# Gated mix of two attentions: the first 512 positions in halves of three tiles, other first loads, and rows whose three parts lie side by side

## The chip, the cores and the metric

The kernel runs on one core of a Trainium2 chip. The metric is the device time of one execution in microseconds (us), as the median of several runs. Engines are named as the profile names them: PE (TensorE, matrix products), PEld (its weight loads), DVE (VectorE), ACT (ScalarE), POOL (GpSimd) and SP (SyncE, which here only issues transfers). A `q` behind an engine's name is its instruction queue. DMA transfers move data between the chip's main memory (DRAM) and the on-chip memory, in which a tile has 128 partitions.

## The reference, cut to what matters

```
x: [2048, 576]; H = 32 heads of Dh = 18
g = sigmoid((x * gate_w).sum(-1))
A: q, k, v = split(x @ wqkv)              # every head has its own q, k, v
   a = concat_heads(softmax(q k^T / sqrt(18)) v) @ wo
B: q = x @ wq;  k = x @ wk;  v = x @ wv   # one k and one v for all 32 heads
   b = concat_heads(softmax(q k^T / sqrt(18)) v) @ wo
out = g * a + (1 - g) * b
```

All of it is in 32-bit floats, with 2048 positions. The two attentions make 64 heads; heads 0 to 31 (B) share one key, heads 32 to 63 (A) have their own.

## The kernel before, in words

**Precision.** A 32-bit value is cut into a high and a low part, each of a format (fp32r) that PE multiplies in one pass. A product of two values is made of three products of parts: high by high, low by high and high by low. For the scores, the parts stand as rows of one matmul: a query's 18 rows three times (high, high, low) and a key's (high, low, high), which gives 54 rows; two further rows carry the row maximum and ones. Each such block is kept twice in a tile, at partitions 0 (`SB`, used for the scores) and 64 (`MB`, used for the search for the maximum), so that PE can work with both halves at once. `load_rows` (line 89) brings these blocks from the DRAM tensor `qk_d`, in six transfers of 18 rows: three parts, twice.

**First phase, the projections.** `wall` holds all weights for keys, gate, shared values and queries as 14 tiles of 128 columns (`MT`); `xT` is x transposed. x and each weight tile have 576 rows; they lie as 5 k-tiles, of which the first four are full and the fifth has 64 rows, held twice (high in the upper half of the partitions, low in the lower). `PROJ` lists the 14 products for one output tile: 4 high by high, 4 low by high, 4 high by low, and 2 on the fifth k-tile. `project(mt, c, w)` makes the tile `mt` for the 512 positions of chunk `c`: 14 matmuls into a PSUM bank (`ps_s`, three banks), then ACT copies the high part, DVE subtracts for the low part, and POOL issues the transfer to `qk_d`. Tile 0 (shared key, gate, shared values) also keeps a plain copy `pst`. For tiles with keys, chunk 1 also gives the difference of keys of chunk 1 and chunk 0 (`pdhl`), written to `kd_d`; in the search for the maximum ACT takes the positive part of what it gives, and DVE adds that to the scores of chunk 0, so that one pass of DVE gives the maximum over both chunks.

**Start.** `load5` loads a block of five k-tiles in three transfers: the first four k-tiles, then the fifth twice, into the two halves. The first weight tile and the first 256 positions of x go out on SP, with their small transfers on ACT (`rest`); then the second 256 positions, weight tiles 1 and 2, and the rest of x in pieces of 512, all on SP. Two pieces of 512 fit at a time; the third waits for the first to be split. PE multiplies dummy data six times meanwhile (line 246). `first_x` (line 215) splits the first weights and the first 256 positions, `split_x` (line 227) any later 256: ACT copies all five k-tiles for the high part, DVE subtracts four for the low part (`low_x`, line 236) and the lower half of the fifth (line 237). Then chunk 0 is made: tile 0 in two halves of 256 positions, tile 1, tile 2; and the same for chunks 1 to 3, each with the splitting of the next 512 positions behind tile 1 and with `shared_v` (four transposes on PE, a copy on DVE) before tile 2. `project_rest` (line 283) makes tiles 3 to 13 and issues, one per call of `project`, the list `rows_back` of first key and query loads.

**Second phase.** For 64 heads and 16 blocks of 128 keys: `step_max` searches the maximum 22 steps ahead, `step_scores` makes the scores and ACT their exponentials, `step_pv` multiplies with the values. The order of all instructions is written out by hand (`manual_schedule`, the strings `PLAIN`, `SPARSE`, `DENSE`, `ALONE`); each engine and each queue works through its own in that order. `load_q`, `load_k` and `next_kd` (`load_kd`, line 97: three transfers of 18 rows) are put on SP at steps given by `when`.

Of the kernel before, what the change touches and what calls it, by code (L numbers as in the profile page):

```python
# [8 lines left out]
F32 = mybir.dt.float32  # L9
# [15 lines left out]
MT = 14  # L25
# [17 lines left out]
def gated_mix_kernel(ctx: ExitStack, tc: tile.TileContext, xT, wall, wv, wo, out):  # L43
# [3 lines left out]
    def dma(o, i, eng=None):  # L47
        o, i = (x.bitcast(F32) if x.dtype == F32R else x for x in (o, i))
        return (eng or nc.sync).dma_start(o, i)
# [91 lines left out]
    def project(mt, c, w, parts=1):  # L141


        fp = ps_s.tile([P, 512], F32, name="ps")
        cs = slice(c * 512, (c + 1) * 512)
        g = 512 // parts
        for i in range(parts):
            for n, (a, b, k, kr) in enumerate(PROJ):
                nc.tensor.matmul(fp[:, g * i:g * i + g], w[a][:kr, k, :],  # L149
                                 X[b][:kr, k, c * 512 + g * i:c * 512 + g * i + g],  # L150
                                 start=(n == 0), stop=(n == len(PROJ) - 1))
        hl = stp.tile([P, 2, 512], F32R, name="phl", bufs=4)
        nc.scalar.activation(hl[:, 0, :], fp, AF.Copy)  # L153
# [5 lines left out]
        nc.vector.tensor_tensor(hl[:, 1, :], fp, hl[:, 0, :].bitcast(F32), op=OP.subtract)  # L159
        dma(qk_d[:, mt * P:(mt + 1) * P, cs].rearrange("a p f -> p a f"), hl, nc.gpsimd)  # L160
        if c == 1 and mt in HAS_K:
            d = stp.tile([P, 512], F32, name="pd", bufs=1)
            nc.vector.tensor_tensor(d, fp, KD.pop(mt), op=OP.subtract)
            dhl = stp.tile([P, 2, 512], F32R, name="pdhl", bufs=1)
            split(d, dhl[:, 0, :], dhl[:, 1, :], nc.scalar, nc.vector)
            dma(kd_d[:, mt * P:(mt + 1) * P, :].rearrange("a p f -> p a f"), dhl, nc.gpsimd)
        if mt == 0:
            dma(z_d[cs], st[ROW_G:ROW_G + 1, :])
            return c, st

    def shared_v(c, st):
        pv = ps_m.tile([P, 512], F32, name="pm")
        for j in range(4):
            nc.tensor.transpose(pv[:, 18 * j:18 * j + 18],  # L174
                                st[ROW_VB:ROW_VB + 18, j * P:(j + 1) * P],
                                ident[ROW_VB:ROW_VB + 18, ROW_VB:ROW_VB + 18])
        nc.vector.tensor_copy(vb[:, 4 * c:4 * c + 4, 0:18],
                              pv[:, 0:72].rearrange("p (j d) -> p j d", d=18))
# [28 lines left out]
    with tc.tile_pool(name="xs", bufs=1, side="right") as xsp:  # L207
        XS = []

        def load_x(c, rest=None):  # L210
            half = c < 2
            XS.append(xsp.tile([P, NKT, 256 if half else 512], F32, name="xsh" if half else "xs", bufs=2))
            load5(XS[c], xT[:, 256 * c:256 * c + 256] if half else xT[:, 512 * (c - 1):512 * c], rest)

        def first_x():

            xs, xh = XS[0], X["h"][:, :, 0:256]
            w = {y: wpool.tile([P, NKT, P], F32R, name=f"w{y}", bufs=3) for y in "hl"}
            st = W.pop(0)
            nc.scalar.activation(w["h"], st, AF.Copy)  # L220
            nc.vector.tensor_copy(xh[:, 0:3], xs[:, 0:3])
            nc.scalar.activation(xh[:, 3:5], xs[:, 3:5], AF.Copy)  # L222
            nc.vector.tensor_tensor(w["l"], st, w["h"].bitcast(F32), op=OP.subtract)
            low_x(0, xs)
            return w

        def split_x(c):
            xs = XS[c // 2 + 1][:, :, 256 * (c % 2):256 * (c % 2) + 256] if c > 1 else XS[c]
            cs = slice(c * 256, (c + 1) * 256)
            nc.scalar.activation(X["h"][:, :, cs], xs, AF.Copy)  # L230
            low_x(c, xs)

        def low_x(c, xs):
            cs = slice(c * 256, (c + 1) * 256)
            xh = X["h"][:, :, cs]
            nc.vector.tensor_tensor(X["l"][:, :, cs], xs[:, 0:4], xh[:, 0:4].bitcast(F32), op=OP.subtract)
            nc.vector.tensor_tensor(xh[64:128, 4], xs[64:128, 4], xh[64:128, 4].bitcast(F32), op=OP.subtract)

        W = [load_w(0, nc.scalar)]
        load_x(0, nc.scalar)  # L240
        nc.scalar.activation(ones, ones, AF.Copy)
        load_x(1)

        warm = ps_m.tile([P, 512], F32, name="pm")
        for i in range(6):
            nc.tensor.matmul(warm[:, 0:304], ident, vb.rearrange("p k d -> p (k d)"), start=True, stop=True)
        W.append(load_w(1))
        W.append(load_w(2))
        for c in range(2, 5):
            load_x(c)  # L250
        dma(ones_r.rearrange("a (b c) -> (a b) c", c=32), ones)
        for mt in range(3, 6):
            W.append(load_w(mt))
        for t in vst:
            nc.gpsimd.memset(t, 1.0)
        WP = [first_x()]
        split_x(1)
        WP.append(prep_w(W.pop(0)))
        WP.append(prep_w(W.pop(0)))
        for c in range(4):  # L260
            keep = project(0, c, WP[0], 2 if c == 0 else 1)
            if c == 3:
                WN = prep_w(W.pop(0))
            project(1, c, WP[1])
            if c < 3:
                split_x(2 * c + 2)
                split_x(2 * c + 3)
            shared_v(*keep)
            project(2, c, WP[2])
    vwp = ph1.enter_context(tc.tile_pool(name="vwp", bufs=1, side="right"))  # L270

    def load_wv(hf):
# [540 lines left out]
```

## Time and profile before

| | before |
|---|---|
| median of 3 runs | 2756.39 us (2756.0 to 2756.66) |
| the profiled execution | 2756.49 us, span 2754.5 us |
| granted TensorE clock, mean | 0.999 |
| HBM read, written | 137.23 MB, 64.77 MB |
| packets on SP's and ACT's transfers, on POOL's | 108880 and 4928, 9504 |

A row of the table of stretches gives a stretch's bounds and length, then for each engine its busy time in it and the number of its instructions, then the granted clock, the mean busy share of the DMA engines and what they moved in GB/s. A row of the timeline gives the start, the duration, the engine with the line of the kernel, the operation, the tile written and the tiles read, and in brackets how long the engine had been idle and what released it. A row of the chain of waits gives start, duration and what held the end back at that time. A matmul's end is modelled, so starts of successive groups are the better measure of its pace.

### The profile page before, as it was taken

What the parts mean: (1) busy time and instruction counts of PE and PEld (TensorE: products, weight loads), DVE (VectorE), ACT (ScalarE), POOL (GpSimd) and SP (SyncE); (2) the same over time, 40 slices, a digit from 0 to 9 for tenths busy, and PEclk for the clock granted to TensorE, in tenths of its full rate; (3) what the DMA queues carried; (4) which work ended last, traced back from release to release, by engine and by line L of the source; (5) the groups of instructions that cost most, each with busy time, mean ns of one, the idle gap of its engine ahead of it and who ended that gap; (6) DMA issues with size and microseconds to landing.
All of it is one profiled execution on the core that took longest, in us unless ns stands there. A gap on an engine that the chain in (4) does not pass through costs nothing.

```text
span 2754.5 us, 59149 instructions
## 1 busy us (share of the span) xinstructions
PE 2744.5 (100%) x22926; PEld 1264.5 (46%) x22926; DVE 2414.4 (88%) x4518; ACT 2432.4 (88%) x4777; POOL 209.3 (8%) x339
## 2 busy tenths in 40 slices
PE   9999999999999999999999999999999999999999
PEld 7888333333333333333334444444444333334554
DVE  4347999999999999999999898888989999998873
ACT  3332999999999999999999999999999999998776
POOL 2220000001000100100110001000100011011000
PEclk9999999999999999999999999999999999999999
DMA  8652011112112111211133323322331233234312
GB/s 265 251 218 72 24 33 27 32 43 66 37 27 57 51 33 35 62 48 28 52 94 107 83 58 96 93 67 77 100 87 47 66 86 97 67 75 123 110 36 88
DMA packets 123592, 214.61 MB, mean 78 GB/s; under 512 B 53516, under 2 KB 81628, under 8 KB 111626
## 3 DMA queue, kind: packets, MB, share of 16 engines
q1 hardware_dynamic: 108880, 171.05, 22.9%
q0 software_dynamic: 9504, 34.61, 3.3%
q10 hardware_dynamic: 4928, 5.18, 0.5%
q8 instruction: 180, 2.95, 0.5%
q14 instruction: 100, 0.82, 0.1%
HBM read 137.23 MB, written 64.77 MB: 73 GB/s over the span
## 4 chain that ended last, share of the span: by engine, by line
PE 99%; DMA 0%; DVE 0%; ACT 0%; issue 0%; SPq 0%
PE acc L430 39%; PE ps L417 37%; PE pm L382 9%; PE ps L149 7%; PE pm L565 4%; PE ps L185 2%; PE pm L417 0%; PE ps L382 0%; DMA xsh<-xT 0%; DVE oacc L574 0%; DMA wst<-wall 0%; DVE mx L391 0%; ACT pt L424 0%; PE ps L619 0%; PE pm L174 0%
## 5 line engine op out<-in xcount | busy, mean ns | idle before, releaser
L424 ACT ACTIVATE pt<-ps 128x512 f32<-128x512 f32 x4052 | 2131.5, 613 | 106.5 <-PE pm L382 45.0
L391 DVE TENSOR_REDUCE mx<-pm 128x1 f32<-128x512 f32 x3064 | 1946.9, 684 | 141.1 <-PE pm L382 100.5
L417 PE MATMUL ps<-qs,ksb 56*128 56x512 f32 x2688 | 905.8, 437 | 0.3
L382 PE MATMUL pm<-ksb,qs 54*128 54x512 f32 x2332 | 806.7, 441 | 0.0
L417 PEld LDWEIGHTS ps<-qs,ksb 56*128 56x128 f32 x2688 | 436.8, 184 | 643.7 <-ACT pt L424 622.8
L430 PE MATMUL acc<-pt,vb 128*19 128x256 f32 (+1 forms) x6144 | 592.4, 457 | 0.0
L430 PE MATMUL acc<-pt,vg 128*19 128x256 f32 (+3 forms) x6432 | 573.9, 443 | 0.5 <-DVE oe L442 0.4
L417 PE MATMUL ps<-qs,ksa 56*128 56x512 f32 x1364 | 453.5, 437 | 0.1
L382 PE MATMUL pm<-ksa,qs 54*128 54x512 f32 x1232 | 425.5, 438 | 0.0
L382 PEld LDWEIGHTS pm<-ksb,qs 54*128 54x128 f32 x2332 | 373.7, 184 | 34.8 <-DVE mx L391 15.2
L388 DVE CUSTOM_DVE_ANT_0 junk<-pm,xb 128x512 bf16<-128x512 f32 x500 | 340.3, 681 | 1.3 <-ACT xb L385 1.2
L417 PEld LDWEIGHTS ps<-qs,ksa 56*128 56x128 f32 x1364 | 218.3, 184 | 245.9 <-ACT pt L424 216.4
L385 ACT ACTIVATE xb<-pm 128x512 f32<-128x512 f32 x500 | 306.2, 612 | 0.0
L382 PEld LDWEIGHTS pm<-ksa,qs 54*128 54x128 f32 x1232 | 197.9, 184 | 56.3 <-DVE mx L391 25.9
L430 PEld LDWEIGHTS acc<-pt,vg 128*19 128x19 f32 x6432 | 122.3, 97 | 216.1 <-issue 190.4
L430 PEld LDWEIGHTS acc<-pt,vb 128*19 128x19 f32 x6144 | 104.3, 97 | 209.5 <-issue 199.0
L382 PE MATMUL pm<-kdb,qs 54*128 54x512 f32 x372 | 150.6, 405 | 0.0
L115 POOL CAST mh<-mt 128x32 fp32r<-128x32 f32 x64 | 13.4, 210 | 1729.1 <-DVE mt L399 1729.0
L153 ACT ACTIVATE phl<-ps 128x512 fp32r<-128x512 f32 x56 | 33.5, 598 | 102.9 <-PE ps L149 74.0
L159 DVE TENSOR_TENSOR phl<-ps,phl 128x512 fp32r<-128x512 f32 x56 | 38.7, 692 | 93.7 <-ACT phl L153 70.9
L149 PE MATMUL ps<-xh,wh 128*128 128x512 f32 (+1 forms) x285 | 83.5, 390 | 2.5 <-ACT xh L222 1.8
L149 PE MATMUL ps<-xh,wl 128*128 128x512 f32 (+1 forms) x285 | 82.7, 388 | 0.0
(118 smaller groups left out, 1370.7 us busy)
## 6 DMA issues: line engine op xcount, KB each, us to landing
qs<-qk SPq DMA_DIRECT2D x384, 144.0 KB
qk<-phl POOLq DMA_DIRECT2D x56, 512.0 KB, 4.3
ksa<-qk SPq DMA_DIRECT2D x132, 144.0 KB
ksb<-qk SPq DMA_DIRECT2D x66, 144.0 KB
onh<-oh SPq DMA_DIRECT2D x32, 256.0 KB
onl<-ol SPq DMA_DIRECT2D x32, 256.0 KB
oih<-onh SPq DMA_DIRECT2D x16, 512.0 KB
oil<-onl SPq DMA_DIRECT2D x16, 512.0 KB
```

The source lines that it names most:

```text
L149: nc.tensor.matmul(fp[:, g * i:g * i + g], w[a][:kr, k, :], X[b][:kr, k, c * 512 + g * i:c * 512 + g * i + g], start=(n == 0), stop=(n == ...
L153: nc.scalar.activation(hl[:, 0, :], fp, AF.Copy)
L159: nc.vector.tensor_tensor(hl[:, 1, :], fp, hl[:, 0, :].bitcast(F32), op=OP.subtract)
L185: nc.tensor.matmul(fp[:, 0:288], X[b][:kr, k, st_ * P:(st_ + 1) * P], w[a][:kr, k, :], start=(n == 0), stop=(n == len(PROJ) - 1))
L382: nc.tensor.matmul(pm, qs[u % 3][b:b + 54, i * P:(i + 1) * P], k, start=True, stop=True)
L385: nc.scalar.activation(MX["x", u, i], pm, AF.Relu)
L388: nc.vector.tensor_tensor_reduce(junk, pm, MX.pop(("x", u, i)), 1.0, -3e38, op0=OP.add, op1=OP.max, accum_out=MX[u][:, i, c:c + 1])
L391: nc.vector.tensor_reduce(MX[u][:, i, c:c + 1], pm, axis=AX.X, op=OP.max)
L417: nc.tensor.matmul(ps, kst(u)[b:b + 56, i * P:(i + 1) * P], qs[u % 3][b:b + 56, c * 512:(c + 1) * 512], start=True, stop=True)
L424: nc.scalar.activation(pt, ps, AF.Exp, scale=SCALE)
L430: nc.tensor.matmul(acc[32 * j:32 * j + 19, a:b], v_of(u, i), PT[u, i, j][:, a:b], start=(i == 0), stop=(i == 15), skip_group_check=True)
L565: nc.tensor.matmul(fp[:, 0:288], x, y, start=(n == 0 and not joins), stop=(n == len(ops) - 1))
```

## The change

There are three edits.

1. **First loads.** Weight tiles 1 and 2 now come ahead of the second 256 positions of x, and the two small transfers of the fifth k-tile of each of these three (`rest`) are issued by POOL instead of SP. The large transfers stay on SP.
2. **First 512 positions.** The splitting of the first three weight tiles and of the first 256 positions is cut into "the first four k-tiles" (`main_w`, first half of the x split, `low_x`) and "the fifth" (`last_w`, `last_x`), and ordered so that the former of all three tiles come first. `project` is cut into `products` (matmuls n0 to n1 of the list) and `leave` (the rest). Chunk 0 is then made with three banks at once: products 0 to 11 for the first 256 positions of tiles 0, 1, 2, then products 12 and 13 of these, then the second 256 positions tile by tile. Tile 0 of chunk 1, instead of chunk 0, is made in two halves.
3. **Rows.** In a block of 54 rows the three parts of a row now lie side by side (row 3d + part instead of 18 part + d): `load_rows` still issues six transfers of 18 rows, each to every third partition. `kd_d` holds the three parts of a row next to each other, so `load_kd` is one transfer of 54 rows; it is written with two transfers (two parts, then the first again) in place of one.

```diff
-    kd_d = dram.tile([2, MT * P, 512], F32, name="kd")
+    kd_d = dram.tile([MT * P, 3, 512], F32, name="kd")
...
-                put(t[b + 18 * i:b + 18 * i + 18, :], qk_d[y, r:r + 18, :])
+                put(t[b + i:b + 54:3, :], qk_d[y, r:r + 18, :])
...
     def load_kd(t, r, put=dma):
-        for i, y in enumerate((0, 1, 0)):
-            put(t[MB + 18 * i:MB + 18 * i + 18, :], kd_d[y, r:r + 18, :])
+        put(t[MB:MB + 54, :], kd_d[r:r + 18, :, :].rearrange("p a f -> (p a) f"))
...
+    def products(fp, w, x0, p0, g, n0=0, n1=len(PROJ)):
+        for n, (a, b, k, kr) in list(enumerate(PROJ))[n0:n1]:
+            nc.tensor.matmul(fp[:, p0:p0 + g], w[a][:kr, k, :], X[b][:kr, k, x0 + p0:x0 + p0 + g],
+                             start=(n == 0), stop=(n == len(PROJ) - 1))
...
-            dma(kd_d[:, mt * P:(mt + 1) * P, :].rearrange("a p f -> p a f"), dhl, nc.gpsimd)
+            dma(kd_d[mt * P:(mt + 1) * P, 0:2, :], dhl, nc.gpsimd)
+            dma(kd_d[mt * P:(mt + 1) * P, 2, :], dhl[:, 0, :], nc.gpsimd)
...
-        def first_x():
...
+        def main_w(st):
+            w = {y: wpool.tile([P, NKT, P], F32R, name=f"w{y}", bufs=3) for y in "hl"}
+            nc.scalar.activation(w["h"][:, 0:4], st[:, 0:4], AF.Copy)
+            nc.vector.tensor_tensor(w["l"][:, 0:4], st[:, 0:4], w["h"][:, 0:4].bitcast(F32), op=OP.subtract)
             return w
+        def last_w(st, w):
+            nc.scalar.activation(w["h"][:, 4], st[:, 4], AF.Copy)
+            nc.vector.tensor_tensor(w["l"][:, 4], st[:, 4], w["h"][:, 4].bitcast(F32), op=OP.subtract)
...
         W = [load_w(0, nc.scalar)]
         load_x(0, nc.scalar)
         nc.scalar.activation(ones, ones, AF.Copy)
-        load_x(1)
+        W.append(load_w(1, nc.gpsimd))
+        W.append(load_w(2, nc.gpsimd))
+        load_x(1, nc.gpsimd)
...
-        W.append(load_w(1))
-        W.append(load_w(2))
         for c in range(2, 5):
             load_x(c)
...
-        WP = [first_x()]
+        x0, xh = XS[0], X["h"][:, :, 0:256]
+        ST = [W.pop(0) for _ in range(3)]
+        WP = [main_w(ST[0])]
+        nc.scalar.activation(xh[:, 0:2], x0[:, 0:2], AF.Copy)
+        nc.vector.tensor_copy(xh[:, 2:4], x0[:, 2:4])
+        low_x(0, x0)
+        WP.append(main_w(ST[1]))
+        WP.append(main_w(ST[2]))
+        last_w(ST[0], WP[0])
+        nc.scalar.activation(xh[:, 4], x0[:, 4], AF.Copy)
+        last_x(0, x0)
+        last_w(ST[1], WP[1])
+        last_w(ST[2], WP[2])
         split_x(1)
-        WP.append(prep_w(W.pop(0)))
-        WP.append(prep_w(W.pop(0)))
+        FP = [ps_s.tile([P, 512], F32, name="ps") for _ in range(3)]
+        for n in ((0, 12), (12, 14)):
+            for mt in range(3):
+                products(FP[mt], WP[mt], 0, 0, 256, *n)
         for c in range(4):
-            keep = project(0, c, WP[0], 2 if c == 0 else 1)
...
+            for mt in range(3):
...
+                if c == 0:
+                    products(FP[mt], WP[mt], 0, 256, 256)
+                    done = leave(mt, c, FP[mt])
+                else:
+                    done = project(mt, c, WP[mt], 2 if c == 1 and mt == 0 else 1)
```

More of the change, by code (lines that the diff above doesn't have):

```diff
@@ L144, in project, with leave @@
         fp = ps_s.tile([P, 512], F32, name="ps")
-        cs = slice(c * 512, (c + 1) * 512)
         g = 512 // parts
         for i in range(parts):
[L148 to L151, printed above, removed]
+            products(fp, w, c * 512, g * i, g)
+        return leave(mt, c, fp)
+    def products(fp, w, x0, p0, g, n0=0, n1=len(PROJ)):
+        for n, (a, b, k, kr) in list(enumerate(PROJ))[n0:n1]:
+            nc.tensor.matmul(fp[:, p0:p0 + g], w[a][:kr, k, :], X[b][:kr, k, x0 + p0:x0 + p0 + g],
+                             start=(n == 0), stop=(n == len(PROJ) - 1))
+    def leave(mt, c, fp):
+        cs = slice(c * 512, (c + 1) * 512)
         hl = stp.tile([P, 2, 512], F32R, name="phl", bufs=4)
@@ L231, in split_x, with last_x @@
             low_x(c, xs)
+            last_x(c, xs)
         def low_x(c, xs):
             cs = slice(c * 256, (c + 1) * 256)
[L235 to L237 removed]
+            nc.vector.tensor_tensor(X["l"][:, :, cs], xs[:, 0:4], X["h"][:, 0:4, cs].bitcast(F32), op=OP.subtract)
+        def last_x(c, xs):
+            xh = X["h"][64:128, 4, c * 256:(c + 1) * 256]
+            nc.vector.tensor_tensor(xh, xs[64:128, 4], xh.bitcast(F32), op=OP.subtract)
         W = [load_w(0, nc.scalar)]
```

24 lines of the change are left out of this document (9 added, 15 removed).

## The prediction

> **What bounds the kernel now.** I read the page's first part, then busy time in stretches cut where the clock or the stage changes, then the chain and the timeline of the first 25 us, last the queue of SP within one head.
>
> ```profile
> span 2754.5 us, 59149 instructions
> ...
> PE 2744.5 (100%) x22926; PEld 1264.5 (46%) x22926; DVE 2414.4 (88%) x4518; ACT 2432.4 (88%) x4777; POOL 209.3 (8%) x339
> ```
> ```profile
> 0.00:7.39 7.39, 5.47 (x11) 3.81 (x12) 0.84 (x3) 2.25 (x3) 1.57 (x9) 1.00 0.66 200
> 7.39:10.81 3.42, 1.13 (x5) 0.47 (x4) 1.68 (x2) 0.52 (x1) 0.00 (x0) 1.00 0.60 148
> 10.81:14.22 3.41, 3.25 (x14) 3.13 (x15) 3.17 (x4) 2.64 (x4) 0.00 (x0) 0.50 0.69 202
> 14.22:22.56 8.34, 8.34 (x45) 6.88 (x45) 4.65 (x7) 4.12 (x5) 1.67 (x2) 1.00 1.03 308
> 22.56:196.00 173.44, 173.44 (x782) 143.51 (x781) 70.97 (x102) 59.00 (x94) 47.07 (x71) 1.00 0.72 255
> 196.00:273.60 77.60, 77.31 (x531) 65.79 (x531) 59.73 (x100) 17.20 (x42) 0.76 (x3) 1.00 0.23 79
> ...
> 277.00:1400.00 1123.00, 1122.96 (x9702) 426.41 (x9702) 1082.70 (x2046) 1102.63 (x2182) 61.56 (x108) 1.00 0.16 42
> 1400.00:2729.00 1329.00, 1328.10 (x11675) 596.00 (x11667) 1173.70 (x2215) 1235.55 (x2432) 93.49 (x142) 1.00 0.30 80
> 2729.00:2754.50 25.50, 21.11 (x162) 17.51 (x160) 15.21 (x40) 6.41 (x15) 3.22 (x4) 1.00 0.49 186
> ```
>
> Columns of the stretches: length, busy time of PE, PEld, DVE, ACT, POOL, granted clock, DMA share, GB/s. PE shows work in all but 10.0 us. Of those 10.0, 4.4 lie in the last 25.5 us, which the change doesn't touch, 1.2 between 196 and 2729 us, where the change touches only loads, and 4.4 before 14.22 us. In that beginning there are two more losses that "busy" hides: 3.41 us at half clock, and about 6 us of matmuls on dummy data (line 246). So the room of this change is the beginning:
>
> ```profile
> 10.97 7.98 PE ps L149 x39
> 18.96 0.35 PE pm L174 x4
> ```
> ```profile
> 1.92 6.02 PE L246 MATMUL pm<-vb,ident 128*128 128x304 f32 x12 [1.92 <-POOL vst L255]
> ...
> 7.51 0.95 DVE L221 CAST xh<-xsh 128x768 fp32r<-128x768 f32 x1 [5.70 <-DMA xsh<-xT]
> 8.38 0.81 DVE L223 TENSOR_TENSOR wl<-wst,wh 128x640 fp32r<-128x640 f32 x1
> ...
> 10.29 0.63 ACT L222 ACTIVATE xh<-xsh 128x512 fp32r<-128x512 f32 x1 [3.30 <-DMA wst<-wall]
> 10.83 1.25 ACT L230 ACTIVATE xh<-xsh 128x1280 fp32r<-128x1280 f32 x1
> 10.96 1.23 DVE L236 TENSOR_TENSOR xl<-xsh,xh 128x1024 fp32r<-128x1024 f32 x1 [1.76 <-ACT xh L222]
> ...
> 11.99 0.72 ACT L125 ACTIVATE wh<-wst 128x640 fp32r<-128x640 f32 x1
> 12.21 0.42 DVE L237 TENSOR_TENSOR xh<-xsh,xh 64x256 fp32r<-64x256 f32 x1
> ...
> 14.40 0.64 PE L149 MATMUL ps<-xh,wl 128*128 128x256 f32 x4
> 14.88 0.64 PE L149 MATMUL ps<-xl,wh 128*128 128x256 f32 x4
> ...
> 15.79 0.60 ACT L153 ACTIVATE phl<-ps 128x512 fp32r<-128x512 f32 x1 [1.97 <-PE ps L149]
> ...
> 16.52 1.07 PE L149 MATMUL ps<-xh,wl 128*128 128x512 f32 x4
> 17.43 1.07 PE L149 MATMUL ps<-xl,wh 128*128 128x512 f32 x4
> ...
> 22.56 1.07 PE L149 MATMUL ps<-xh,wh 128*128 128x512 f32 x4
> ```
>
> DVE can use the first four k-tiles of the first x at 7.51, but ACT waits until 10.3 for the fifth, whose half rows come by ACT's queue. (Its row names wst; line 222 reads only xsh, so it is that transfer.) From 10.97 PE works without a gap: the first 512 positions of three tiles are done at 22.56. From there on PE has no gap to the end of the projections, so a time won before 22.56 is won at the end.
>
> **The change, part by part.** *First stage.* What must be done before 22.56 is 6 half tiles of 14 products and 4 transposes. Two groups of 4 products of 256 columns start 0.48 us apart (14.40, 14.88), so 0.12 us each at full clock; of 512 columns 0.91 us apart (16.52, 17.43), so 0.227 us each.
>
> Start: the first four k-tiles of x are there at 7.5 as before, since they still follow only the first weights on SP's queue; for the small transfers that POOL now adds beside them I allow 0.2. Half of xh is 512 columns on each of ACT and DVE, 0.63 (line 222), so PE starts at 8.35. The first weights no longer wait for their half rows, which leaves the path. 8 products end at 9.3; DVE's low part (0.64 cast, then 1.23) is ready at 9.6, so 12 products end at 10.05. The next two tiles take 12 x 0.12 each if their weights are split by then: their low parts, 0.65 each on DVE (0.81 x 512/640) behind 0.58 each for the high parts on ACT (0.72, line 125, x 512/640), are needed at 10.5 and 12.0, so the first must have landed by 9.3 and the second by 10.7. Then 12.9, and the 6 products on the fifth k-tile, here by 10.3 and split by 12, end at 13.65.
>
> ```profile
> 9.73 1.58 SPq L49 DMA_DIRECT2D wst<-wall  x3
> ```
> ```profile
> SPq L49 <- DMA xsh<-xT: 1.7, 1, 1.7
> ```
> ```profile
> 1.01 0.29 POOL masks.py:199 TENSOR_SCALAR_AFFINE_SELECT ident<-ident 128x128 f32<-128x128 f32 x1
> ...
> 17.91 0.93 POOL L49 DMA_DIRECT2D qk<-phl  x1 [15.73 <-DVE phl L159]
> ```
> ```profile
> L49 POOL DMA_DIRECT2D kd<-pdhl x10: 725/725/727, 30.0 to 190.1; - x10
> ...
> DMA to landing us min/median/max: 3.2/3.4/7.8
> ```
>
> Second half: it needs the third weights and then the second x, which now stands behind both weight tiles. On SP issue was slow before: the third tile's weights went out at 9.73, after a wait of 1.7 for an earlier transfer, with six small transfers ahead of them. These six go to POOL now, so SP issues all its large ones by about 4.5 and the DMA engines always have work. By bytes: three weight tiles (320 KB each) and two x (640 KB each) are 2.29 MB; 1.48 MB moved by 7.39 before (200 GB/s), the other 0.81 take 2.6 us at 308 GB/s or 5.5 at 148: the second x lands between 10.0 and 12.9, the weights some 2 us before. I take 11, nearer to the fast row, since 148 GB/s was SP waiting. POOL is free at 1.3; six issues of 0.73 to 0.93 start the last at 4.9 to 5.9; with 3.2 to 7.8 to landing, the fifth k-tile of the second x is there at 8.1 to 13.7; with the median 3.4, at 9. ACT is done with the weights by 12, splits x to 13.2, DVE to 14.5 and 14.9. PE starts the second half at 13.65, needs the low part at 14.6, and ends its first tile at 15.35. The two others 1.68 each, the transposes 0.35: **19.05 against 22.56, 3.5 us won**. Of a landing after 12 about each us is lost; an earlier one wins nothing.
>
> *Priced losses.* Two halves instead of one matmul in the first tile of the next 512 positions: 28 x 0.12 against 14 x 0.227, 0.2 lost. Splitting the third and fourth 256 positions (1.25 on ACT, 1.65 on DVE each) had the 6.7 us of two tiles of 512 columns and the transposes; now it has 3.7. ACT gets to it 0.6 (line 153) after the second tile's end (17.05): high part 18.9, low 20.1, last 20.5, then 20.1, 21.8, 22.2; PE needs these at 19.05, 20.0, 20.6, 20.8, 21.8, 22.3. So 0.1. The clock: after the stretch 7.39 to 10.81, with PE busy a third of it, 3.41 us ran at half. PE is now busy 0.55 (dummies), 0.95 and 1.2 of it, 80%; the rows have no such case between 33% (half follows) and 95% (10.81 to 14.22, full follows). Half again costs 1.6 of the 3.2 us of work; none costs 0. I count 0.6: nearer to the busy row, but the stretch can lie otherwise in the next run. **Sum: 3.5 - 0.2 - 0.1 - 0.6 = 2.6 us won.** Bounds: 3.8 (start at 8.15, then 84 x 0.12 and 0.35 without a wait, less 0.2) and 1.4 (landing at 13.7: PE's first tile then ends at 17.0, which hides the clock's loss).
>
> [...] If the move brought no bytes earlier, x would land at 12.9 and the sum be 1.9.
>
> *Rows side by side, one transfer of key differences.* Same bytes, same number of q and k transfers, same matmul shapes (54 rows): nothing changes for PE, ACT, DVE. A head issues one kd load instead of three.
>
> ```profile
> 2002.58 1.16 SPq L49 DMA_DIRECT2D kda<-kd  x3
> 2003.78 9.52 SPq L49 DMA_DIRECT2D qs<-qk  x6
> 2013.35 2.19 SPq L49 DMA_DIRECT2D ksa<-qk  x6
> ...
> 2026.48 0.32 SPq L49 DMA_DIRECT2D onl<-ol  x1
> 2039.59 0.32 SPq L49 DMA_DIRECT2D m_d<-mh  x1
> ```
>
> That frees 0.8 us a head on SP, which stands idle from 2026.8 to 2039.6 in this head, so nothing: the cover is that idle time, and PE's 1.2 us of gaps between 196 and 2729 are all that faster loads could win. On POOL ten key tiles get a second write, 10 x 0.73 us plus 2.6 MB, in a stage where POOL is busy 47 of 173 us and PE never stops: nothing. Without that cover it would be 7 us.
>
> **The forecast** is 2754.5 - 2.6 = 2751.9 for the span; the profiled run was 2756.5 around a span of 2754.5, within 0.1 of the median 2756.39, so 2753.8 for the median.
>
> **Rivals.** (1) *Nothing stands in the way*: no half clock and no wait, 3.2 to 3.8 won: 2753.2 to 2752.6, I put 2753.0. For it: 80% busy. Against: the loads have 0.5 to 1 us of room at each step.
>
> (2) *The fifth k-tile of the second x comes late, slower than before*: ACT splits all five k-tiles in one instruction, so 128 KB on POOL's queue hold the whole second half. It decides from a landing at about 15.3, where nothing is won; at 17 it is 1.7 slower: 2758.1. For it: POOL's first issue took 0.93, one of its transfers took 7.8 to land, and its queue has to share the engines with SP's, which is now never empty. Against: 13.7 is the worst sum of the rows.
>
> (3) *Interleaved rows taken for overlapping*: the three parts now lie at every third partition. If the order of writes is kept by their outer bounds, each waits for the one before: 8 waits a head where q and k are both loaded.
>
> ```profile
> 20.95 1.23 DVE L236 TENSOR_TENSOR xl<-xs,xh 128x1024 fp32r<-128x1024 f32 x1 [0.63 <-ACT xh L230]
> 21.19 1.08 PE L149 MATMUL ps<-xl,wh 128*128 128x512 f32 x4
> ```
>
> Against: here DVE writes 256 positions of xl in four pieces while PE reads other positions between these pieces, so strides are told apart, at least within a partition. Price: at 3.4 us to landing less 0.3 of issue, 8 x 3.1 = 25 us a head; SP's idle 12.8 and most of the 8 that it already waits within the q load (9.52 for six issues that take about 2) cover 20. It decides from 20 / 8 = 2.5 us a wait. 5 us over, for 31 heads: +155, if the next head's maximum waits for all; I put +60, about 2816.
>
> **How the numbers follow.** The forecast (1.2 to 3.2 won) 0.60; (1) 0.16; (2) and lesser gains 0.14; (3) 0.05; 0.05 for what I don't see. Range 2752.5 to 2757.5: below lies a start that no row allows, above the worst of (2), and (3). About 0.2%, 5.5 us, is what a measurement of this kernel can tell from no change. The forecast, (1) and (2) lie inside it, and the beginning's own room, 4.0, is less, so faster has only part of the unseen, 0.03. Slower: (3) and the rest, 0.09. Same 0.88.
>
> **What would show it.** Right: products of 256 columns start near 8.4, no wait for line 222's fifth k-tile, the first 512 positions end at 19 to 21, and from there all is shifted by the same amount. The loads: the third weights issued before 5, ACT's high part of the second x begun at 11 to 12. The clock: a stretch at 0.50, or none, near 10.8. Part two: one kd issue a head, and PE's busy share from 277 to 2729 unchanged. The prediction is wrong if ACT starts that high part after 14, if PE waits for SP's loads anywhere later, or if SP shows waits between the three parts of a row.

## The result, and the profile after

| | before | after |
|---|---|---|
| median, lowest and highest | 2756.01 us (2754.60 to 2758.02, 18 runs) | 2751.41 us (2750.54 to 2753.11, 18 runs) |
| ratio after to before, 95% interval | | 0.9984 [0.9977, 0.9991] |
| span of the profiled execution | 2754.5 us | 2750.5 us |

The changed kernel is 4.6 us faster by the medians, 4.0 by the spans; the prediction had 2.6, and its range ended at 2752.5. The start gave what was forecast. The rest came from where the prediction put "nothing". Leads and lengths of heads below are read from one profiled execution of each kernel, and that one can lie over 1 us from the median (for the changed kernel 2752.82 against 2751.41).

The page after, its first lines, and busy time by stretch (columns as before; 269.05 and 275.88 are the bounds of the stretch at half clock):

```profile
span 2750.5 us, 59178 instructions
...
PE 2741.8 (100%) x22968; PEld 1264.3 (46%) x22968; DVE 2413.1 (88%) x4521; ACT 2432.6 (88%) x4781; POOL 216.8 (8%) x355
```
```profile
0.00:7.39 7.39, 5.44 (x12) 3.50 (x12) 1.67 (x5) 2.17 (x4) 4.98 (x15) 1.00 0.70 195
7.39:10.81 3.42, 2.83 (x19) 2.46 (x20) 2.54 (x4) 2.12 (x5) 0.00 (x0) 1.00 1.05 276
10.81:14.22 3.41, 3.41 (x31) 3.41 (x30) 2.21 (x6) 1.81 (x4) 0.00 (x0) 1.00 1.07 343
14.22:22.56 8.34, 8.29 (x67) 7.78 (x66) 5.51 (x8) 4.49 (x6) 1.49 (x2) 1.00 0.93 289
...
196.00:269.05 73.05, 72.75 (x508) 62.80 (x506) 56.96 (x96) 14.94 (x37) 0.76 (x3) 1.00 0.22 73
269.05:275.88 6.83, 6.83 (x28) 2.94 (x31) 3.72 (x8) 4.99 (x12) 0.00 (x0) 0.50 0.03 10
275.88:1400.00 1124.12, 1124.04 (x9714) 426.89 (x9706) 1083.14 (x2047) 1102.90 (x2185) 61.73 (x108) 1.00 0.15 43
1400.00:2725.00 1325.00, 1324.27 (x11669) 593.91 (x11665) 1171.06 (x2212) 1234.52 (x2429) 93.70 (x142) 1.00 0.27 80
```

In the beginning the half clock at 10.81 is gone and the transfers run at 276 and 343 GB/s, where they had run at 148 and 202. From 275.88 to 2725 PE is busy all but 0.8 us (0.9 before, from 277 to 2729). By busy time the second phase shows no difference at all, so it has to be read by when the same piece of work happens. Each of the 64 heads has one DVE transpose of its row maxima. Here are those of heads 0, 1, 30 and 63 from the timeline, first before, then after:

```profile
248.66 0.21 DVE L399 STREAM_TRANSPOSE mt<-m 128x32 f32<-128x32 f32 x1
294.27 0.21 DVE L399 STREAM_TRANSPOSE mt<-m 128x32 f32<-128x32 f32 x1
1368.43 0.21 DVE L399 STREAM_TRANSPOSE mt<-m 128x32 f32<-128x32 f32 x1
2681.95 0.21 DVE L399 STREAM_TRANSPOSE mt<-m 128x32 f32<-128x32 f32 x1
```
```profile
245.97 0.21 DVE L429 STREAM_TRANSPOSE mt<-m 128x32 f32<-128x32 f32 x1
292.37 0.21 DVE L429 STREAM_TRANSPOSE mt<-m 128x32 f32<-128x32 f32 x1
1366.64 0.21 DVE L429 STREAM_TRANSPOSE mt<-m 128x32 f32<-128x32 f32 x1
2677.30 0.21 DVE L429 STREAM_TRANSPOSE mt<-m 128x32 f32<-128x32 f32 x1
```

The lead is 2.69 at head 0, 1.90 at head 1, 1.79 at head 30, 4.65 at head 63, and 4.0 at the end. So 0.8 is lost where the second phase begins (the clock, 6.83 us at half instead of 3.41), 2.86 is won over the heads with their own keys, and 0.65 is lost after the last head.

The 2.86 grow evenly, by about 0.1 us a head, at one place of each: where PE multiplies the first query block with a new head's key differences. The timeline of PE there, before and then after:

```profile
2190.70 0.50 PE L417 MATMUL ps<-qs,ksa 56*128 56x512 f32 x1
2190.71 0.49 PE L382 MATMUL pm<-ksa,qs 54*128 54x512 f32 x1
2191.04 0.39 PE L417 MATMUL ps<-qs,ksa 56*128 56x512 f32 x1
2191.17 0.46 PE L382 MATMUL pm<-kda,qs 54*128 54x512 f32 x1
2191.56 0.63 PE L430 MATMUL acc<-pt,vg 128*19 128x256 f32 x8
```
```profile
2187.05 0.50 PE L447 MATMUL ps<-qs,ksa 56*128 56x512 f32 x1
2187.05 0.49 PE L412 MATMUL pm<-ksa,qs 54*128 54x512 f32 x1
2187.39 0.39 PE L447 MATMUL ps<-qs,ksa 56*128 56x512 f32 x1
2187.41 0.47 PE L412 MATMUL pm<-kda,qs 54*128 54x512 f32 x1
2187.81 0.63 PE L460 MATMUL acc<-pt,vg 128*19 128x256 f32 x8
```

A score (`ps`, with operands at the partitions from 0) and a search for the maximum (`pm`, from 64) start together, at 2190.70 and 2190.71 in the first pair before. Before, the matmul on `kda` started 0.13 behind its partner, and the products with the values 0.52 behind it; after, 0.02 and 0.42. No row says that anything waited, since PE's pieces follow each other without a gap.

The trace also has records that these views leave out: semaphore instructions in PE's weight-load sequence. Between the two pairs above they stand like this (start, duration):

```
before                                    after
2190.845 0.051 semaphore                  2187.190 0.051 semaphore
2190.849 0.185 weights of ps<-qs,ksa      2187.194 0.183 weights of ps<-qs,ksa
2190.956 0.051 semaphore                  2187.301 0.051 semaphore
2191.062 0.051 semaphore                  2187.377 0.183 weights of pm<-kda,qs
2191.137 0.183 weights of pm<-kda,qs
```

They follow each other at 0.106 to 0.111 us. Each of these instructions names two semaphores, and the load of the weights of `pm<-kda,qs` one. By the programs' listings, the matmul on `kda` waits for seven semaphores before (three transfers of the query block's upper half, three of the key differences, DVE) and for five after (one transfer of key differences). Three semaphore instructions became two. That is the first theory, W: **what PE waits for, counted at that one matmul, costs PE time, although all of it arrived long ago.** (The prediction's rows have the loads of a head's key differences leave SP at 2002.58; the matmul on them runs at 2037.1, and the trace's last landing on the six semaphores of transfers that it waits for is at 2029.72.)

### The profile page after: what moved, and what is told of

Read it like the earlier page. It is cut to its first block, busy times and chain, and to the rows that moved or that the text cites. A ratio compares the mean times of both kernels' runs of the same rounds, so it can differ in the third digit from the quotient of the medians.

```text
span 2750.5 us, 59178 instructions
## 1 busy us (share of the span) xinstructions
PE 2741.8 (100%) x22968; PEld 1264.3 (46%) x22968; DVE 2413.1 (88%) x4521; ACT 2432.6 (88%) x4781; POOL 216.8 (8%) x355
## 4 chain that ended last, share of the span: by engine, by line
PE 98%; DVE 1%; DMA 1%; SPq 0%; ACT 0%; issue 0%; DVEq 0%; ACTq 0%
PE acc L460 38%; PE ps L447 36%; PE pm L412 9%; PE ps L153 6%; PE pm L595 4%; PE ps L192 2%; DVE mx L421 1%; DMA xsh<-xT 0%; PE pm L447 0%; PE ps L412 0%; DMA R<-r_d 0%; DMA r_d<-sm 0%; SPq L49 0%; DVE oacc L604 0%; DVE junk L418 0%
```

## The experiments

Each ratio is to runs of the kernel before that were taken together with the run: medians 2756.50 us for e1 to e4, 2756.66 for e5 to e8, 2756.06 for e9 to e12. An interval reaches about 0.09%, 2.4 us, to either side, so the times alone tell few of these kernels apart, and the argument goes by the traces. Where a table gives "a head", it is the mean time from a head's first exponential to the next head's, heads 50 to 56, from the starts of ACT's exponentials; "step 10" is the median of the step with the matmul in question among a head's 16 steps, in the same heads.

**e1 and e2: the two halves of the change alone.** e1 is the changed kernel with the rows and key differences of before; e2 is the kernel before with those of the change (the same lines the other way round).

```diff
 e1, against after
-    kd_d = dram.tile([MT * P, 3, 512], F32, name="kd")
+    kd_d = dram.tile([2, MT * P, 512], F32, name="kd")
...
-                put(t[b + i:b + 54:3, :], qk_d[y, r:r + 18, :])
+                put(t[b + 18 * i:b + 18 * i + 18, :], qk_d[y, r:r + 18, :])
...
-        put(t[MB:MB + 54, :], kd_d[r:r + 18, :, :].rearrange("p a f -> (p a) f"))
+        for i, y in enumerate((0, 1, 0)):
+            put(t[MB + 18 * i:MB + 18 * i + 18, :], kd_d[y, r:r + 18, :])
...
```

> The first two edits alone; rows and key differences as before (three transfers of key differences a head). Theory W (what PE waits for): the gain of the second phase comes from the number of semaphores that the first matmul on a head's key differences waits for, 7 before and 5 after, at about 0.055 us for each beyond 5. Here they are 7 again, so only the start's 2.7 us are won: about 2753.4; the tenth step of a head (heads 50 to 56) takes 2.36 us as before, and the first 512 positions end near 19.5 as after. Rival S (the start alone carries it, the rest is luck of the profiled run): about 2751.4, the tenth step 2.25.

Measured: 2755.10 us, ratio 0.9995 [0.9986, 1.0003]. Its transposes of heads 30 and 63:

```profile
1366.95 0.21 DVE L429 STREAM_TRANSPOSE mt<-m 128x32 f32<-128x32 f32 x1
2680.54 0.21 DVE L429 STREAM_TRANSPOSE mt<-m 128x32 f32<-128x32 f32 x1
```

It leads the kernel before by 1.48 at head 30 and 1.41 at head 63: over the own-key heads the start wins nothing. The half clock near 269 lasts 6.83 us in it too.

> The third edit alone; the start as before. Theory W: 5 semaphores, the tenth step of own-key heads 2.25 us, 30 heads x 0.1: 2.8 won, about 2753.2; the first 512 positions end at 22.56. Rival S: nothing won, 2756.0.

Measured: 2754.29 us, ratio 0.9991 [0.9982, 1.0000]:

```profile
1369.19 0.21 DVE L399 STREAM_TRANSPOSE mt<-m 128x32 f32<-128x32 f32 x1
2680.00 0.21 DVE L399 STREAM_TRANSPOSE mt<-m 128x32 f32<-128x32 f32 x1
```

0.76 behind at head 30, 1.95 ahead at head 63: 2.71 won there by the rows alone. The total times lie above what W forecast for either (2753.4 and 2753.2) and decide nothing; what is missing in the profiled executions lies before head 30 and after head 63, not in these heads.

**e3, e4, e5, e9: how many semaphores.** The changed layout stays; only the number of transfers of key differences differs, with the same bytes: three, five, two, four.

```diff
-        put(t[MB:MB + 54, :], kd_d[r:r + 18, :, :].rearrange("p a f -> (p a) f"))
+        a = 0
+        for n in (6, 6, 6):           # e4: (4, 4, 4, 3, 3), e5: (9, 9), e9: (5, 5, 4, 4)
+            put(t[MB + 3 * a:MB + 3 * (a + n), :], kd_d[r + a:r + a + n, :, :].rearrange("p a f -> (p a) f"))
+            a += n
```

> The changed kernel, but a head's key differences come in three transfers of 18 rows (six rows with their three parts each): same layout, same bytes, rows still side by side. Theory W: 7 semaphores, so the tenth step is 2.36 again and 2.8 to 3.3 us are lost against the changed kernel: about 2754.5. Rival R (the layout, rows side by side or the strided writes, or the fewer bytes in flight, is what helps): 2751.4, the tenth step 2.25.

> The changed kernel, but a head's key differences come in five transfers (4, 4, 4, 3 and 3 rows with their three parts). Theory W: 9 semaphores, four beyond 5, 4 x 0.055 = 0.22 us a head, 30 heads: 6.6 us lost against the changed kernel, about 2758; the tenth step 2.47. Rival R: 2751.4, the tenth step 2.25. If only being over a limit counts and not how many: like three transfers, about 2754.5.

> The changed kernel with a head's key differences in two transfers of 9 rows each; the first matmul on them waits for 6 semaphores, between the 5 of the changed kernel and the 7 of before. Theory W (each semaphore beyond five that this one matmul waits for costs about 0.055 us): step 10 of a head 2.30 against 2.247 (one transfer) and 2.351 (three), a head 37.10 against 37.043 and 37.154, 1.6 us lost over heads 32 to 61, so some 1.6 above the changed kernel, 2753.0. Rival R (three parts a row or the number of transfers from three on): 2.25, 2751.4. Rival T (a threshold at more than five): 2.35 at once, 2754.5.

> The changed kernel with a head's key differences in four transfers of 5, 5, 4 and 4 rows; the first matmul on them waits for 8 semaphores. Theory V (the matmul keeps one wait itself, the others go in pairs, each pair a semaphore instruction of about 0.107 us in TensorE's sequence ahead of it; the first two such instructions are covered, from the third on each delays the pair of matmuls): 8 semaphores make 4 of them, as 9 did, so step 10 and its neighbour as with five transfers, a head 37.26 in heads 50 to 57, and 2758 to 2759. Theory W (0.055 us for each semaphore beyond five, already contradicted by two transfers costing what three do): a head 37.20, 2757.

Measured, in the order of the semaphores for which the matmul waits (by the listings); the semaphore instructions are those that the trace has between the two pairs in heads 52 and 54; the lead is that on the kernel before, by the transposes of heads 30 and 63:

| | semaphores | semaphore instructions | a head | lead won in heads 30 to 63 | median | ratio |
|---|---|---|---|---|---|---|
| after | 5 | 2 | 37.043 | +2.86 | 2751.41 | 0.9984 [0.9977, 0.9991] |
| e2 | 5 | 2 | 37.061 | +2.71 | 2754.29 | 0.9991 [0.9982, 1.0000] |
| e5 | 6 | 3 | 37.161 | +0.06 | 2754.87 | 0.9994 [0.9985, 1.0003] |
| before | 7 | 3 | 37.163 | 0 | 2756.01 (with after) | 1 |
| e1 | 7 | 3 | 37.167 | -0.07 | 2755.10 | 0.9995 [0.9986, 1.0003] |
| e3 | 7 | 3 | 37.154 | +0.36 | 2755.58 | 0.9996 [0.9987, 1.0005] |
| e9 | 8 | 4 | 37.256 | -2.73 | 2757.64 | 1.0005 [0.9996, 1.0013] |
| e4 | 9 | 4 | 37.261 | -2.80 | 2758.80 | 1.0008 [0.9999, 1.0017] |

e3 and e4 spoke for W, with 0.055 us a semaphore. e5 contradicted this form of it: with six the cost was that of seven, as rival T had it, and e4's nine cost more again, so it goes in steps. The records give the step: the number of semaphore instructions, which is (semaphores - 1) / 2, rounded up. That is theory V, and e9 was made to test it: eight semaphores cost what nine do (37.256 against 37.261), not the 37.20 of W. (Its median, 2757.64, lies between the forecasts of W, 2757, and V, 2758 to 2759, and decides nothing.) The fourth instruction shows in the step before step 10 more than in step 10, where W had looked for it: 2.56 us instead of 2.47 there, 2.38 instead of 2.35 here. The layout of the rows is no cause: e3, e4, e5 and e9 have that of the change. In e4's timeline the matmul on `kda` is 0.25 behind its partner, where it was 0.13 and 0.02:

```profile
2189.84 0.39 PE L450 MATMUL ps<-qs,ksa 56*128 56x512 f32 x1
2190.09 0.47 PE L415 MATMUL pm<-kda,qs 54*128 54x512 f32 x1
```

Most of these waits are for transfers, six of the seven before and four of the five after. The runs give the price: the third and the fourth such instruction cost 0.10 to 0.12 us a head each, about the 0.106 to 0.111 at which they follow each other.

**e8: the waits on two instructions.** e3 with a tiny matmul on the key differences half a head ahead, so that from head 34 on no matmul on them waits for more than four semaphores.

```diff
+    def touch(u):
+        k = L["kd", u][MB:MB + 54, :]
+        nc.tensor.matmul(ps_m.tile([P, 512], F32, name="pm")[0:32, 0:16], k[:, 0:32], k[:, 0:16], start=True, stop=True)
+
+    for u in range(H + 2, NU):
+        when(16 * (u - 2) + 8, lambda u=u: touch(u))
```

> The kernel of e3 (key differences in three transfers, seven semaphores at the first matmul on them) with one tiny matmul more a head, 32 by 16, that reads the key differences of the head after next half a head ahead and so takes three of the waits on itself. Theory W as the number of waits at one instruction: step 10 of a head 2.25 to 2.27 as in the changed kernel, a head 37.04 to 37.10 with the tiny matmul's 0.01 to 0.06, 2751.4 to 2753.0. Rival: the waits cost wherever they stand, or it is the data that come late: step 10 2.35, a head 37.15 to 37.2, 2754.5 to 2756.

Measured: 2757.08 us, ratio 1.0003 [0.9994, 1.0012]; a head 37.183. The rival came nearer: nothing is won by moving the waits along PE's sequence. Step 10 itself fell only from 2.351 to 2.311; two semaphore instructions now stand ahead of the tiny matmul, its step grew from 2.146 (after) to 2.273, and steps 8 to 10 together take 6.99 us against 6.98 in e3. These heads show the loss too small: the lead on the kernel before falls from 3.17 at head 30 to 0.27 at head 63, by 2.90, as much as in e4 and e9, most of it in heads 32 to 49 at 0.13 a head. With two semaphore instructions at either matmul e8 has four in all, as e4 and e9 have. How much of the loss is the tiny matmul itself, the run doesn't tell.

**e10: five semaphores in the old layout.** e1 with every block of three parts loaded in two transfers, one of two parts and one of one (`load_rows` and `load_kd` call `two`).

```diff
+    def two(t, b, src, r, first, put):
+        d = t[b:b + 36, :]
+        if first == "hh":
+            put(d, src[0:1, r:r + 18, :].to_broadcast([2, 18, src.shape[2]]))
+            put(t[b + 36:b + 54, :], src[1, r:r + 18, :])
+        else:
+            put(d, src[0:2, r:r + 18, :])
+            put(t[b + 36:b + 54, :], src[0, r:r + 18, :])
...
```

> The kernel of e1 (the changed start; rows in blocks of 18 as before) with each block of three parts loaded in two transfers, of two parts and of one: the key differences are in two transfers, and so are q and k; the first matmul on the differences waits for 5 semaphores. Theory V: two semaphore instructions, so step 10 of a head 2.25 as in the changed kernel though the rows lie as before: a head 37.04 against e1's 37.167, some 2.8 to 3.7 us under e1 at the end of the heads, 2751 to 2752. Rival (it is the rows side by side that win): step 10 2.36, a head 37.16, 2755.

Measured: 2855.45 us, ratio 1.0359 [1.0345, 1.0373]. Step 10 is 2.251, as V had it, with the rows as before: the layout isn't needed for the gain. But PE now stands still 15 times for over 0.5 us, 68 us in all, and is busy 31 us longer than in e1 (2776.5 against 2745.4) at a mean clock of 0.981: together the 99 us between the two spans. SP's queue for the same piece of a head, e10 and then e1:

```profile
2218.80 2.19 SPq L49 DMA_DIRECT2D ksb<-qk  x4
2223.72 18.54 SPq L49 DMA_DIRECT2D ot<-oe  x8
```
```profile
2167.88 2.37 SPq L49 DMA_DIRECT2D ksb<-qk  x6
2172.87 6.44 SPq L49 DMA_DIRECT2D ot<-oe  x8
```

The eight issues behind the key load take 18.54 us instead of 6.44, and everything behind them on SP comes late. While these loads run the DMA engines are nearly idle, 0.16 busy and 59 GB/s:

```profile
2230.00:2236.00 6.00, 6.00 (x56) 2.25 (x54) 5.80 (x11) 5.95 (x13) 0.00 (x0) 1.00 0.16 59
```

In the packet records, packets of 8 KB overlap two at a time there (time of the packets over time elapsed: 2.0 to 2.1 from 2227 to 2235), against nine at a time in e1 (9.0 to 9.1 from 2168 to 2174, at a DMA share of 0.54 from 2168 to 2173). So where sources of 2 by 18 rows are in the queue, two packets move at a time, and nine where all are of 18 rows; the records don't name the DMA engine, and why it is two and nine no run shows. One more thing shows here: heads below 32, whose matmul at this place now waits for three semaphores (one instruction instead of two), take 36.995 us against 37.046 after (means of heads 2 to 27). So the second instruction doesn't seem to be hidden entirely either: 0.05, by this one run, whose other loads of queries and keys are fewer too.

**e6: the fifth k-tile of the second 256 positions apart.** This asks whether rival 2's transfer held ACT at 12.18.

```diff
-        split_x(1)
+        nc.scalar.activation(X["h"][:, 0:4, 256:512], XS[1][:, 0:4], AF.Copy)
+        low_x(1, XS[1])
+        nc.scalar.activation(X["h"][:, 4, 256:512], XS[1][:, 4], AF.Copy)
+        last_x(1, XS[1])
```

> The changed kernel with the second 256 positions split in two steps: k-tiles 0 to 3 high and low, then the fifth. If the fifth k-tile on GpSimd's queue was what ScalarE waited for at 12.18 (rival 2 of the prediction), ScalarE begins the high part of k-tiles 0 to 3 before 12.0 and the next 512 positions begin 0.2 to 0.5 us earlier than at 19.46. If the large transfer on SyncE's queue was last, it begins again at 12.1 to 12.3, and only the shorter instruction (1.0 for 1.27) and TensorE's 0.26 of waiting at 14.76 can be won: 19.2 to 19.3. Either way too little for the time to tell: 2751.4 less 0 to 0.5.

Measured: 2751.82 us, ratio 0.9983 [0.9974, 0.9992]. In its timeline the part that doesn't read the fifth k-tile waited 0.81 for a transfer all the same, and the fifth waited for none:

```profile
11.53 1.06 ACT L279 ACTIVATE xh<-xsh 128x1024 fp32r<-128x1024 f32 x1 [0.81 <-DMA xsh<-xT]
...
12.50 0.40 ACT L281 ACTIVATE xh<-xsh 128x256 fp32r<-128x256 f32 x1
```

The large transfer was last here, not POOL's. In the trace after, POOL's two transfers of this fifth k-tile went out at 3.77 and 4.29 and landed 6.5 and 7.5 us later, so by 11.8, where the prediction had 9: just before ACT began at 12.18. The first products began at 6.51 here and at 7.93 after, so the second 256 positions have to be compared by length: 5.78 us from the first half's end (12.84) to the next 512 positions (18.62), against 5.87 after. The edit is worth 0.1. The start itself differs more by run: over the twelve kernels with the changed start the next 512 positions begin between 18.62 and 19.85.

**e7, e11, e12: the half clock at 269.** Eight scores stand there in a row, and ACT takes one about every half microsecond (ten in 5.23 us in the timeline after), so PE, which needs 0.24 for one (a score and the matmul behind it start 0.24 apart in e12), works half of the time. Theory C: this is what halves the clock. The rival in the expectations below speaks of a window, a piece of 3.41 us: the two stretches at half clock of the kernel before last that long and begin at 10.81 and 273.63, 262.8 us apart, 77.0 times 3.413. Each of the three adds matmuls whose results nobody reads: e7 eight of the identity into the search's banks; e11 (on e6) eight of 54 by 512 into the bank of the value products, not yet in use; e12 as e11, with three more.

```diff
 e7, on the changed kernel
-    emit("ssss ssss")
+    fill = ps_m.tile([P, 512], F32, name="pm")
+    for _ in range(8):
+        emit("s")
+        nc.tensor.matmul(fill[:, 0:128], ident, ident, start=True, stop=True)
 e11 and e12, on e6
+    def fill():
+        nc.tensor.matmul(acc, ksb[SB:SB + 54, 0:128], ksb[SB:SB + 54, 512:1024], start=True, stop=True, skip_group_check=True)
+
-    emit("ssss ssss")
+    for _ in range(8):
+        emit("s")
+        fill()
+    for op in ("sm", "sy", "sm"):     # this and the rest in e12 alone
+        emit(op)
+        fill()
+    emit("4 sm sm sm 2 sm sx 2")
```

> The changed kernel with eight matmuls of the identity by itself (128 columns, about 0.06 us each at full clock), one behind each of the first eight scores of the second phase, whose results nobody reads. Theory C (the half clock at 269 to 276 follows from a TensorE that stands still between short pieces there): the half clock is gone, 1.7 to 3.4 us of work at full instead of half clock, less 0.3 for the eight matmuls where TensorE would have worked: 0.8 to 1.8 won, 2749.6 to 2750.6, and the maximum tile of head 0 at the same time, later ones earlier by this. Rival: the half clock follows from something that eight short matmuls do not change (the window's place by luck): 3.41 to 6.83 us at half again and 2751.4 to 2751.8.

> The kernel of e6 with eight matmuls of 54 by 512 into a PSUM bank that is not yet in use, one behind each of the first eight scores of the second phase, in the same half of the array as these; nobody reads the results. Unlike in e7 they wait for nothing. Theory C (the half clock near 270 follows from TensorE being paced by ScalarE there, 0.23 us of work in each 0.6): TensorE then works 0.46 of each 0.6; the half clock shrinks from 6.83 to 3.41 us or goes, and the tile of head 1's maximum comes 0.5 to 2.5 us earlier than in e6: 2749.5 to 2751.3. Rival (the place of the windows decides, or the time after the scores): 6.83 us at half again and 2751.8.

> As e11, with three more such matmuls in the next three scores, before the first product with the values. Theory C: no half clock near 270 at all, 1.7 to 3.4 us won against e6, less up to 0.7 for the three: 2749 to 2750.8. Rival as in e11: 2751.8 to 2752.5.

Measured: e7 2759.20 us, 1.0009 [1.0001, 1.0018]; e11 2750.72 us, 0.9979 [0.9970, 0.9988]; e12 2751.36 us, 0.9984 [0.9975, 0.9992]. The stretch 270 to 275 in e6, e11 and e12:

```profile
270.00:275.00 5.00, 5.00 (x25) 1.84 (x27) 2.94 (x6) 3.15 (x8) 0.00 (x0) 0.50 0.00 0
```
```profile
270.00:275.00 5.00, 5.00 (x33) 1.89 (x31) 3.38 (x7) 3.73 (x8) 0.00 (x0) 0.72 0.00 0
```
```profile
270.00:275.00 5.00, 5.00 (x45) 2.28 (x42) 3.63 (x7) 4.61 (x11) 0.00 (x0) 1.00 0.00 0
```

All three show PE "busy" 5.00 of 5.00, at 25, 33 and 45 matmuls. With all eleven, the clock stays full: from head 0's transpose to head 1's it takes 44.23 us (245.52 to 289.75), 46.35 in e6 (245.15 to 291.50), so 2.1 us hang on it. That fits theory C, but doesn't show it: e11's 3.41 us at half are also what e3, e4, e5, e8 and e9 have without any filler, and e12 is one profiled execution. e7 had the same aim and lost, by its own filler: the banks weren't free, PE waited 1.28 us for DVE, each filler took 0.42 us at full clock where 0.06 was expected, and 10.24 us ran at half clock. In these 10.24 us the rows show PE busy throughout (3.40 of 3.40, 3.43 of 3.43, 3.41 of 3.41), so standing still, as the rows show it, isn't all that counts. e11's interval ends at 0.9988 and overlaps that of the change: it is the fastest median, but 0.7 us isn't told from the changed kernel.

e12's 2.1 us don't show in its median. Its eleven executions fall into two groups, eight at 2750.5 to 2751.5 us and three at 2753.3 to 2754.0; the profiled one is of the first, so whether the clock stayed full in the others isn't known. The end has a part in it too. There DVE's last addition ends 3.69 us before the span does in the kernel before, 4.34 after, 4.98 in e11 and 5.20 in e12. The last rows of DVE and SP before, after and in e12:

```profile
2749.92 0.85 DVE L574 TENSOR_TENSOR oacc<-pm,oacc 128x288 f32<-128x288 f32 x2
...
2750.43 1.08 SPq L49 DMA_DIRECT2D out<-oacc  x2
```
```profile
2745.27 0.85 DVE L604 TENSOR_TENSOR oacc<-pm,oacc 128x288 f32<-128x288 f32 x2
...
2745.79 1.16 SPq L49 DMA_DIRECT2D out<-oacc  x2
```
```profile
2742.70 1.25 DVE L607 TENSOR_TENSOR oacc<-pm,oacc 128x288 f32<-128x288 f32 x3
...
2743.19 2.21 SPq L49 DMA_DIRECT2D out<-oacc  x3
```

SP's last issue ends 0.74, 0.83 and 1.45 us after DVE; the remaining 2.9, 3.5 and 3.8 pass behind it. Before and after, 1.85 and 2.42 of them go by until the trace's last landing (2753.36 and 2749.37), and 1.10 and 1.09 until the end, with semaphore instructions and drains on the engines. Why these differ between kernels was not tried and stays open.

## Why the prediction was wrong

**The step that failed** is the costing of the single transfer: "That frees 0.8 us a head on SP, which stands idle from 2026.8 to 2039.6 in this head, so nothing: the cover is that idle time". The idle time of SP is right, but SP isn't where a transfer costs. By the listings each transfer is also a semaphore that its reader waits for, and in the records these waits are instructions in PE's sequence, 0.106 to 0.111 us apart, while PE is busy all but 0.9 us from 277 to 2729. Two semaphores fewer take one such instruction of 0.10 to 0.11 us out of each of some 28 heads: 2.86 in the trace, where the prediction put nothing. e2 (the rows alone: 2.71), e3 (three transfers again: 0.36 left) and e4 (five: 2.80 lost) show it. The bound "PE's 1.2 us of gaps between 196 and 2729 are all that faster loads could win" was wrong for the same reason: busy time counted a partner that started 0.13 us late as work. "PE's busy share from 277 to 2729 unchanged" came true and proved nothing.

SP itself was misread too. The same head's loads after the change:

```profile
1999.29 1.20 SPq L49 DMA_DIRECT2D kda<-kd  x1
2000.55 10.54 SPq L49 DMA_DIRECT2D qs<-qk  x6
2011.13 4.33 SPq L49 DMA_DIRECT2D ksa<-qk  x6
```

The one issue of key differences takes 1.20 us here, where the three took 1.16 (0.45 against 1.14 in the next head), and the six issues of keys, now to every third partition, take 4.33 instead of 2.19 (2.37 for six in e1, with rows as before). The change costs SP more time than it frees; what SP's idle time covers is this.

**The start** was right in its mechanism and nearly in its sum. From the timeline after:

```profile
7.93 0.74 PE L153 MATMUL ps<-xh,wh 128*128 128x256 f32 x4 [0.58 <-ACT xh L269]
...
12.18 1.27 ACT L236 ACTIVATE xh<-xsh 128x1280 fp32r<-128x1280 f32 x1 [0.83 <-DMA xsh<-xT]
...
13.59 0.65 PE L153 MATMUL ps<-xh,wh 128*128 128x256 f32 x4
...
14.76 0.74 PE L153 MATMUL ps<-xl,wh 128*128 128x256 f32 x4
...
19.46 0.64 PE L153 MATMUL ps<-xh,wh 128*128 128x256 f32 x4
```

- First products at 7.93 (8.35 predicted), first half of three tiles done at 13.59 (13.65). The loads left SP as forecast: the third weights behind 1.92, the second x at 3.77.
- The second x came at 12.1 instead of 11, inside the bounds 10.0 to 12.9, and held ACT to 12.18. So the next 512 positions begin at 19.46 instead of 19.05: 3.1 won, not 3.5. By e6 it was the large transfer, so rival 2's mechanism had no part in it, though the fifth k-tile came 2.8 later than reckoned.
- Tile 0 of the next 512 positions lost 0.42, against 0.2 and 0.1 priced.
- The half clock at 10.8 didn't come (0.6 had been set aside). That makes 2.69 at head 0, where the sum had 2.6: two errors that cancel.
- What the prediction didn't have is the other end of the clock: 6.83 us at half at 269, where before had 3.41, took 0.8 back. It doesn't follow from the change: e3, e4, e5, e8 and e9 have the same start and 3.41, e1 and e6 have 6.83. The half clock begins at 268.13 to 269.39 where it lasts 6.83 and at 269.99 to 270.88 where it lasts 3.41. In e2, which has the start of before, the granted clock is 0.65 from 10.81 to 14.22 and 0.94 from 14.22 to 22.56, where before has 0.50 and 1.00. So the place differs by run; the prediction had allowed for that ("the stretch can lie otherwise in the next run") at only one of the two places.
- The end cost another 0.65 that no part of the forecast named.

**Rivals.** (1), no wait and no half clock at the start, came half true. (2) had no part in the delay of 12.18. (3) fell: the six issues of keys follow each other at 0.72 us with no wait between a row's three parts, and e2's rows win 2.71.

The result is "no change" by the 0.2% that the prediction named (0.16%), and yet the interval excludes none: with 18 runs the measurement told more than the prediction assumed.

## What to carry to other kernels

Where an engine never stops, count the semaphores at each of its instructions: here a tile brought in more pieces cost PE 0.05 to 0.12 us a head for each two semaphores more, though its loads left SP some 34 us ahead (2002.58 against 2037.1 in one head). Save transfers by a layout in DRAM that makes one long row list, as here for the key differences, not by sources of 2 by 18 rows, with which here two packets moved at a time and the run took 100 us longer (e10 against e1); and look at what the new issues cost (0.72 us each to every third partition, 0.36 to neighbouring ones). And where busy time is 100%, compare the starts of the same work in both traces before you write "nothing": here PE was idle for 0.9 us of the second phase with the pair 0.13 us apart, and for 0.8 with it 0.02 apart.

## What the runs showed of the hardware that was not expected

- Waits beyond the first on the matmul on a head's key differences came in pairs as instructions of their own, 0.106 to 0.111 us apart; 3, 4 or 5, 6 or 7, 8 or 9 semaphores gave 1, 2, 3 and 4 of them. The second seems to cost about 0.05 us a head (one run), the third and fourth 0.10 to 0.12 each.
- The clock was halved for one, two or three times 3.41 us after a stretch whose busy time hardly shows a gap (0.3 us from 196 to 269.05 after); in the one profiled execution with eleven matmuls more there, about 0.24 us each, it wasn't halved. In e7 it stayed at half for 10.24 us in which the rows show PE busy throughout.
- An issue by SP of 18 rows to every third partition took 0.72 us, to 18 neighbouring ones 0.36 (4.33 and 2.19 for six).
